# Batch 1's k and q between the halves of w_out, an earlier gate for w_in, and stores on SyncE: chunked attention with a snake MLP on one core

## The chip, the core and the metric

The kernel runs on one core of a Trainium2 chip. The metric is device time in microseconds (us), from the first to the last instruction of the core. Before the change the median of three runs is 218.45 us (217.29 to 218.61). Profiles are single executions with the hardware profiler on; that of the kernel before spans 218.0 us.

The engines are TensorE (PE in the profile; its weight loads are PEld), VectorE (DVE), ScalarE (ACT), GpSimd (POOL) and SyncE (SP). SyncE issues transfers only. GpSimd issues transfers too, and all loads that convert float32 to bf16 go through it. Each of the two has one queue of its own, in program order: an instruction that waits holds all behind it.

## The reference

Four batches of eight heads attend in chunks of 32 queries, each to 16 positions to the left, 8 to the right and 8 memory positions. The result, as 3072 rows of 512, goes through two matrix products with a "snake" function between them.

```python
def _attn_ref(q, k, v, mem_k, mem_v):          # q, k, v: (4, 8, 768, 64); mem: (4, 8, 8, 64)
    chunk, left_ctx, right_ctx = (32, 16, 8)
    scale = 1.0 / np.sqrt(D)
    for c in range(S // chunk):
        ...                                     # l_start, r_end: the chunk with its context
        k_full = np.concatenate([mem_k, k[:, :, l_start:r_end]], axis=2)
        v_full = np.concatenate([mem_v, v[:, :, l_start:r_end]], axis=2)
        scores = scale * np.matmul(q_c, k_full.transpose(0, 1, 3, 2))
        a = np.exp(scores - scores.max(-1, keepdims=True))
        out[:, :, c_start:c_end] = np.matmul(a / (a.sum(-1, keepdims=True) + 1e-09), v_full)

def _moe_ref(x, w_in, w_out, alpha):            # x: (3072, 512), w_in: (512, 2048), w_out: (2048, 512)
    h = x @ w_in
    s = np.sin(alpha * h)
    return (h + s * s / (alpha + 1e-09)) @ w_out
```

## The kernel before

The program runs batch by batch: attention of batch 0, layer 0 (the first product and the snake), then for each later batch its attention, into which the second product of the batch before is fed a few matmuls at a time, and its layer. Attention works in 8 blocks of 96 queries. The order of instructions is set by hand.

Attention of batch 0, with the gate for the weights and the later loads (cut):

```python
def attention_first(kq, alphas, ahead, load_weights, next_loads):
    ...
    pv(0, 0)
    put_k_edges(0, 2, t2)
    turn_q(2)                       # PE transposes, VectorE copies group 2 into qTs[0]
    warm(1)                         # a matmul of zeros that keeps TensorE busy
    pv(0, 1)
    t3 = turn(kq[0], 3, None)
    put_k(0, 3, t3)
    warm(1)
    x(0, 0)                         # PE transposes, ScalarE copies into xT[0]
    load_weights(xT)
    ...
    pv(1, 1)
    next_loads()
    ...
    ahead(0, xT, (4, 1))            # first half of the first product for groups 0, 1, 2
    ...
    ahead(2, xT, (0, 3))

def load_weights(xT):
    nc.gpsimd.tensor_copy(gate[:], xT[0][0:1, 0, 0:1])   # GpSimd waits for x(0, 0)'s copy
    for c in range(5):
        load_w_in(c)                # columns 0, 256, 512, 1024, 1536 to 2048 of w_in

def next_loads():
    for c in range(2):
        load_w_out(c)               # rows 0-1023, rows 1024-2047
    nc.gpsimd.dma_start(memv_st[64:72, 1:B].rearrange(...), mem_v[1:B].rearrange(...))
    kq1.extend(alloc_qk())
    load_qk(1, kq1, 0, H)           # k of batch 1, then q
```

What layer 0 starts besides its own work, and the way into batch 1's attention:

```python
def send_memv(b):                   # memory rows of v, one copy for each of 8 blocks
    for j in range(NJ):
        nc.sync.dma_start(vws[b % 2][64:72, :, j, 0:D], memv_st[64:72, b])

def begin_0(ft):
    if ft == 3:
        plan(h=[6] + rings["big"])
    if ft == 8:
        load_v(1)
    if ft == 12:
        send_memv(1)
        send_memv(2)
    if ft == 15:
        prs.extend(pair_up(kq1[n // HP], n % HP) for n in range(4))   # GpSimd copies of k

layer(0, xT, "PPPAVPAVAAVAVAAA", begin_0, 0)      # ends with second(0, ...) queued, cut = 13
last4 = rings["h"]
plan(one=(last4[0], last4[0] + 1), t=(last4[1], last4[1] + 1), big=last4[1:])
put_memk(1)
feed.take(20)                       # 20 matmuls of the second product
for pc in range(2 * HP):            # turn k's four pairs, then q's, 2 matmuls after each
    ...
nc.scalar.preload_act_table(ACTF.Exp)
load_v(2)
feed.take(4)
xT = attention(1, feed, (6, 8, 4, 4, 4, 3, 3, 3, 3, 2), 2, 5)
```

The attention of batches 1 to 3. `big` is a ring of three pairs of PSUM banks, which the scores of one block and the values of another take in turn:

```python
def attention(b, stream, shares, lag, crossed, ...):
    state["attending"] = True
    state["store"] = nc.gpsimd
    for s in range(NJ + lag + 1):
        if s < NJ:
            ptl[s] = scores(b, s)                  # 8 matmuls into a pair; ScalarE: exp
        stream.take(n // 2)
        j = s - lag
        state["copying"] = j >= NJ - 1
        if j >= NJ - 1:
            state["store"] = nc.sync
        ...
        if 0 <= j < NJ:
            xbl[j] = values(b, j, ptl.pop(j))      # 8 matmuls into a pair; VectorE: reciprocal, multiply
            if j < crossed:                        # blocks 0 to 4
                nc.sync.dma_start_transpose(block_of(xT, j), ...)
        stream.take(n - n // 2)
        ...

def end_o(s, bank):                                # end of 128 rows of the second product
    o_sb = mlp.tile([P, d_model], F32, name="o_sb", bufs=2)
    if (s % 2 == 0 or state["attending"]) and not state["copying"]:
        nc.vector.tensor_copy(o_sb[:], ps[:, bank, :])
    else:
        nc.scalar.copy(o_sb[:], ps[:, bank, :])
    state["store"].dma_start(out[...], o_sb[:])
```

`state["store"]` is SyncE at first. Layer 2 sets it to GpSimd at its step 12, ahead of batch 3's attention, in both kernels.

Of the kernel before, what the change touches and what calls it, by code (L numbers as in the profile page):

```python
# [9 lines left out]
P = 128  # L10
# [32 lines left out]
def kernel(  # L43
# [12 lines left out]
    nc = tc.nc  # L56
    B, H, S, D = q.shape
# [40 lines left out]
    def single(kind="one"):  # L98
        return ps[:, take_bank(kind), :]

    def packed(bank, n, width):
        return bank.bitcast(BF)[:, 0:n * width].rearrange("p (n c) -> p n c", n=n)
# [8 lines left out]
    qTs = [consts.tile([P, HP, S], BF, name=f"qT{i}") for i in range(2)]  # L111
# [11 lines left out]
    gate = consts.tile([1, 1], BF, name="gate")  # L123
# [6 lines left out]
    def alloc_qk():  # L130
        kb = qkst.tile([P, H, 6, D], BF, name="k_bf")
        qb = qkst.tile([P, H, 6, D], BF, name="q_bf")
        return kb, qb
# [37 lines left out]
    def load_qk(b, bufs, h0, h1):  # L171
        for src, dst in ((k, bufs[0]), (q, bufs[1])):
            nc.gpsimd.dma_start(
                dst[:, h0:h1].rearrange("p h r d -> p h (r d)"),
                src[b, h0:h1].rearrange("h (p r) d -> p h (r d)", p=P),
            )
# [49 lines left out]
    def load_w_out(c):  # L226
        nc.gpsimd.dma_start(
            w_out_sb[:, 8 * c:8 * c + 8, :],
            moe_w_out[1024 * c:1024 * c + 1024].rearrange("(ft p) o -> p ft o", p=P),
        )  # L230
# [10 lines left out]
    def turn(src, hp, pr):  # L241
        t = packed(single("t"), 6, P)
        for r in range(6):
            if pr is not None:
                nc.tensor.transpose(t[:, r, :], pr[:, r].rearrange("p e d -> p (e d)"), ident[:])  # L245
            else:
                for e in range(2):
                    nc.tensor.transpose(  # L248
                        t[64 * e:64 * e + 64, r, :], src[:, 2 * hp + e, r, :], ident[:]
                    )  # L250
        return t

    def put_k_edges(b, hp, t):
        kT = kTs[b % 2]
        for t0, c0 in ((0, 16), (120, 800)):
            nc.vector.tensor_copy(
                kT[:, hp, c0:c0 + 48].rearrange("p (a r) -> p a r", r=6),
                t[:, :, t0:t0 + 8].rearrange("p r a -> p a r"),
            )

    def put_k(b, hp, t):
        kT = kTs[b % 2]
        nc.scalar.copy(  # L263
            kT[:, hp, 72:72 + 7 * 104].rearrange("p (s c) -> p s c", c=104)[:, :, 0:96]
            .rearrange("p s (a r) -> p s a r", r=6),
            t[:, :, 8:120].rearrange("p r (s a) -> p s a r", a=16),
        )

    def put_q(b, hp, t, scalar=False):
        (nc.scalar.copy if scalar else nc.vector.tensor_copy)(  # L270
            qTs[b % 2][:, hp, :].rearrange("p (a r) -> p a r", r=6),
            t.rearrange("p r a -> p a r"),
        )
# [3 lines left out]
    state = {"n": 0, "attending": False, "copying": False, "store": nc.sync}  # L277
# [46 lines left out]
    def alloc_x():  # L324
        return [xp.tile([P, KT, HALF], BF, name=f"xT{hf}") for hf in range(2)]
# [15 lines left out]
    def warm(n):  # L341
        z = ps[:, rings["one"][0], :]
        for _ in range(n):
            nc.tensor.matmul(z, idle[:, 0:P], idle[:])  # L344
# [53 lines left out]
    def attention_first(kq, alphas, ahead, load_weights, next_loads):  # L398
        xT = alloc_x()
        pt, xb = {}, {}  # L400

        def turn_k(hp):
            t = turn(kq[0], hp, None)
            put_k(0, hp, t)
            put_k_edges(0, hp, t)

        def turn_q(hp):
            put_q(0, hp, turn(kq[1], hp, None))

        def sc_half(hp, half):  # L410
            pt[hp, half] = unit_scores(hp, half)

        def sc(hp):
            for half in range(2):
                sc_half(hp, half)

        def pv(*u):
            xb[u] = unit_values(*u, pt[u])

        def x(hp, half, copy=nc.scalar.copy):  # L420
            unit_turn(xT, hp, half, xb.pop((hp, half)), copy)

        turn_k(0)
        warm(2)
        turn_q(0)
        mt = packed(single(), HP, 32)
        for g in range(HP):
            nc.tensor.transpose(mt[:, g, :], memk_bf[0:32, 2 * g:2 * g + 2, :].rearrange("p e d -> p (e d)"), ident[0:32, 0:32])
        nc.vector.tensor_copy(memkT[:], mt)
        put_memk(0)  # L430
        warm(3)
        turn_k(1)
        put_memv(0, nc.vector, 0, H)
        warm(2)
        sc(0)
        turn_q(1)
        alphas()
        warm(3)
        sc(1)
        t2 = turn(kq[0], 2, None)  # L440
        put_k(0, 2, t2)
        pv(0, 0)
        put_k_edges(0, 2, t2)
        turn_q(2)
        warm(1)
        pv(0, 1)
        t3 = turn(kq[0], 3, None)
        put_k(0, 3, t3)
        warm(1)
        x(0, 0)  # L450
        load_weights(xT)
        sc_half(2, 0)
        put_k_edges(0, 3, t3)
        turn_q(3)
        sc_half(2, 1)
        x(0, 1)
        warm(1)
        plan(big=(4, 0, 2))
        pv(1, 0)
        sc_half(3, 0)  # L460
        pv(2, 0)
        sc_half(3, 1)
        pv(3, 0)
        x(1, 0)
        warm(1)
        x(2, 0)
        pv(1, 1)
        next_loads()
        warm(2)
        x(3, 0)  # L470
        nc.scalar.preload_act_table(ACTF.Sin)
        plan(big=(0, 2))
        pv(2, 1)
        ahead(0, xT, (4, 1))
        x(1, 1)
        pv(3, 1)
        ahead(1, xT, (5, 2))
        x(2, 1)
        ahead(2, xT, (0, 3))
        plan(big=(4, 0, 2))  # L480
        x(3, 1, nc.vector.tensor_copy)
        for ft in range(3):
            half_sine(ft, "PVP"[ft])
        return xT

    def attention(b, stream, shares, lag, crossed, beside=iter(()), beside_from=0):
        xT = alloc_x()
        ptl, xbl = {}, {}
        state["attending"] = True
        state["store"] = nc.gpsimd  # L490
        for s in range(NJ + lag + 1):
            n = shares[s] if s < len(shares) else 0
            if s < NJ:
                ptl[s] = scores(b, s)
            if s == NJ - 1:
                nc.scalar.preload_act_table(ACTF.Sin)
            stream.take(n // 2)
            if s >= beside_from:
                next(beside, None)
# [4 lines that stand above are left out]
            if j == NJ:  # L504
                ahead(1, xT)
                half_sine(1)
            if 0 <= j < NJ:
                xbl[j] = values(b, j, ptl.pop(j))
                if j < crossed:
                    nc.sync.dma_start_transpose(  # L510
                        block_of(xT, j), xbl.pop(j)[:].rearrange("p g e d -> p (g e d)")
                    )
            stream.take(n - n // 2)
            if j == NJ - 1:
                ahead(0, xT)
                half_sine(0)
            if crossed <= j - 1 < NJ:
                turn_x(xT, j - 1, xbl.pop(j - 1))
        ahead(2, xT)
        half_sine(2)  # L520
        state["attending"] = state["copying"] = False
        return xT
# [173 lines left out]
    for vw in vws:  # L696
        nc.vector.memset(vw[:, :, :, D:D + 1], 1.0)

    def load_weights(xT):
        nc.gpsimd.tensor_copy(gate[:], xT[0][0:1, 0, 0:1])  # L700
        for c in range(5):
            load_w_in(c)

# [4 lines left out]
        nc.vector.reciprocal(inv_alpha[:], alpha_sb[:])  # L708

    def next_loads():  # L710
        for c in range(2):
            load_w_out(c)
        nc.gpsimd.dma_start(memv_st[64:72, 1:B].rearrange("n b h d -> n (b h) d"),
                            mem_v[1:B].rearrange("b h n d -> n (b h) d"))
        kq1.extend(alloc_qk())
        load_qk(1, kq1, 0, H)

    feed = Feed()
    kq1 = []
    xT = attention_first(kq, alphas, ahead, load_weights, next_loads)  # L720


# [27 lines left out]
# [5 lines that stand above are left out]
        if ft == 12:  # L755
            send_memv(1)
            send_memv(2)
        if ft == 15:
            prs.extend(pair_up(kq1[n // HP], n % HP) for n in range(4))

    layer(0, xT, "PPPAVPAVAAVAVAAA", begin_0, 0)
# [18 lines left out]
    xT = attention(1, feed, (6, 8, 4, 4, 4, 3, 3, 3, 3, 2), 2, 5)  # L780

    for i in range(1, B):
# [28 lines left out]
        if not last:  # L811
# [3 lines left out]
            xT = attention(i + 1, feed, (4, 8, 4, 4, 3, 3, 3, 3, 4, 4, 4), 2, 5)  # L815
# [33 lines left out]
```

The softmax here doesn't subtract the row's maximum and nothing guards it: scores larger than these inputs give would overflow.

## Time and profile before

| What | Value |
|---|---|
| Time, median of 3 | 218.45 us |
| PE busy | 208.4 us |
| ACT busy | 154.2 us |
| DVE busy | 138.0 us |
| POOL busy | 82.5 us |
| POOL queue (q0): bytes moved | 16.64 MB in 71,792 packets |
| SP queue (q1): bytes moved | 10.03 MB in 26,328 packets |
| w_in loads issued by GpSimd | from 18.11 us |
| Batch 1's attention, first scores | 59.20 us |
| Batch 2's attention, first scores | 96.35 us |
| Output stores on SP / on POOL | 18 / 7 |

How to read the profile: a line of a timeline or of a chain of waits starts with the start in us from the beginning and the length in us, then the engine, the line of the kernel and the operation, as output<-input. "x16" is the number of instructions merged into the line. What stands in brackets is how long the engine was idle before, and what it had waited for. In a table of waits the numbers are the total in us, the number of times, and the longest. SPq and POOLq are the queues that issue transfers, which are not counted as busy time on SP. A DMA issue has the time to landing beside it: from the issue until all of it has arrived. Busy time of PE includes overlap of one matmul with the next, so small holes matter more than the percentage suggests.

### The profile page before, as it was taken

Reading aid. Unit: us, or ns where it says so; the run is one execution under the profiler, and the core shown is the slowest. Engines: PE = TensorE matmul, PEld = TensorE weight load, DVE = VectorE, ACT = ScalarE, POOL = GpSimd, SP = SyncE. Lnnn points to the kernel's source line nnn. Section 1 sums busy time; section 2 is a strip of 40 time slices with the busy share of each in tenths; the row PEclk is TensorE's granted clock in tenths of the full one; section 3 lists DMA queues with packets and bytes.
Section 4 is the critical chain, followed back from the end, with each engine's and each line's share of the span. In section 5 each row is a group of like instructions: output and inputs, shape, how many; then the busy total and the mean of one; then the engine's idle time right before and its main releaser. Section 6 shows DMA issues by size and latency. Waiting matters only on the chain.

```text
span 218.0 us, 4433 instructions
## 1 busy us (share of the span) xinstructions
PE 208.4 (96%) x1660; PEld 114.3 (52%) x1684; DVE 138.0 (63%) x246; ACT 154.2 (71%) x241; POOL 82.5 (38%) x108
## 2 busy tenths in 40 slices
PE   7989799999999999989999999999999999999994
PEld 2456556555545655644555555544555555544453
DVE  5767679994527789985756675665853753871110
ACT  2357879994778999998968778897876778651010
POOL 7987696208811599401168199111000000000000
PEclk9999999999999999999999999999999999999999
DMA  5999999999999599998529999997510110111212
GB/s 78 166 162 139 154 205 204 202 205 161 144 186 177 113 125 151 160 163 119 119 34 168 117 122 148 179 250 132 120 51 2 48 53 0 48 48 51 96 48 96
DMA packets 98141, 26.94 MB, mean 124 GB/s; under 512 B 86520, under 2 KB 95624, under 8 KB 98120
## 3 DMA queue, kind: packets, MB, share of 16 engines
q0 software_dynamic: 71792, 16.64, 89.0%
q1 hardware_dynamic: 26328, 10.03, 24.7%
q8 instruction: 13, 0.21, 0.4%
q14 instruction: 8, 0.07, 0.2%
HBM read 29.66 MB, written 6.29 MB: 165 GB/s over the span
## 4 chain that ended last, share of the span: by engine, by line
PE 74%; DVE 8%; ACT 6%; DMA 6%; issue 4%; POOL 0%; DVEq 0%; ACTq 0%
PE ps L597 33%; PE ps L528 28%; DVE gT L582 4%; ACT u L538 4%; DMA w_in_sb<-in_moe_w_in_dram 4%; PE ps L344 3%; PE ps L284 3%; PE ps L310 2%; DMA xT<-x_blk 2%; DVE u L552 2%; PE ps L620 2%; PE ps L248 1%; ACT kT L263 1%; PE ps L245 1%; DVE qT L270 1%
## 5 line engine op out<-in xcount | busy, mean ns | idle before, releaser
L597 PE MATMUL ps<-w_out_sb,gT 128*128 128x512 bf16 x347 | 91.6, 380 | 1.6 <-DVE gT L582 0.4
L528 PE MATMUL ps<-xT,w_in_sb 128*128 128x384 bf16 x512 | 90.9, 326 | 1.7 <-DMA w_in_sb<-in_moe_w_in_dram 1.0
L582 DVE SCALAR_TENSOR_TENSOR gT<-u,inv_alpha,ps 128x768 bf16<-128x768 f32 (+1 forms) x76 | 65.6, 885 | 19.8 <-ACT u L549 16.3
L538 ACT ACTIVATE u<-ps,alpha_sb 128x768 f32<-128x768 f32 (+1 forms) x76 | 59.6, 794 | 18.9 <-PE ps L528 18.5
L528 PEld LDWEIGHTS <-w_in_sb 128*128 128x128 bf16 x512 | 49.5, 98 | 38.3 <-issue 1.6
L597 PEld LDWEIGHTS <-gT 128*128 128x128 bf16 x368 | 32.7, 97 | 29.8 <-issue 1.3
L549 ACT ACTIVATE u<-u 128x768 f32<-128x768 f32 (+1 forms) x50 | 37.0, 741 | 1.6
L297 ACT ACTIVATE pt<-ps,biasm 128x256 bf16<-128x256 f32 x72 | 28.7, 472 | 5.0 <-PE ps L284 2.1
L610 DVE COPY o_sb<-ps 128x512 f32<-128x512 f32 x14 | 9.6, 689 | 26.7 <-PE ps L597 26.7
L613 POOL DMA_DIRECT2D out_dram<-o_sb x7 | 4.0, 569 | 41.4 <-DVE o_sb L610 25.2
L552 DVE TENSOR_TENSOR u<-u 128x768 f32<-128x768 f32 (+1 forms) x20 | 17.9, 893 | 1.7 <-ACT u L538 1.6
L184 POOL DMA_DIRECT2D vw<-in_v_dram x15 | 18.0, 1213 | 0.9 <-issue 0.9
L317 DVE TENSOR_TENSOR x_blk<-ps,rinv 96x512 bf16<-96x512 f32 x24 | 16.5, 687 | 0.8
L612 ACT COPY o_sb<-ps 128x512 f32<-128x512 f32 x9 | 5.2, 580 | 12.9 <-PE ps L597 12.9
L263 ACT COPY kT<-ps 128x672 bf16<-128x672 bf16 x8 | 5.7, 717 | 10.7 <-PE ps L248 7.9
L142 POOL DMA_DIRECT2D kst<-in_k_dram x16 | 11.3, 705 | 4.4 <-DMA vw<-in_v_dram 4.4
L147 POOL DMA_DIRECT2D kst<-in_k_dram x16 | 11.8, 740 | 0.5 <-DMA qst<-in_q_dram 0.3
L310 PEld LDWEIGHTS <-pt 128*128 128x128 bf16 x192 | 9.1, 98 | 4.3
L152 POOL DMA_DIRECT2D qst<-in_q_dram x12 | 10.9, 911 | 1.0 <-DMA vw<-in_v_dram 1.0
L284 PEld LDWEIGHTS <-kT 64*128 64x128 bf16 x192 | 4.9, 94 | 10.4 <-issue 9.5
L344 PE MATMUL ps<-idle 128*128 128x512 bf16 x24 | 8.9, 497 | 1.5 <-DVE vw L659 1.2
L316 DVE RECIPROCAL rinv<-ps 96x8 f32<-96x8 f32 x24 | 4.8, 202 | 8.2 <-ACT pt L297 5.2
(83 smaller groups left out, 146.2 us busy)
## 6 DMA issues: line engine op xcount, KB each, us to landing
out_dram<-o_sb SPq DMA_DIRECT2D x16, 256.0 KB
w_out_sb<-in_moe_w_out_dram POOLq DMA_DIRECT2D x2, 1024.0 KB, 19.5
out_dram<-o_sb POOLq DMA_DIRECT2D x7, 256.0 KB, 3.4
w_in_sb<-in_moe_w_in_dram POOLq DMA_DIRECT2D x3, 512.0 KB, 11.3
vw<-in_v_dram POOLq DMA_DIRECT2D x3, 512.0 KB, 8.9
qst<-in_q_dram POOLq DMA_DIRECT2D x12, 128.0 KB, 6.3
vw<-in_v_dram POOLq DMA_DIRECT2D x2, 448.0 KB, 17.4
kst<-in_k_dram POOLq DMA_DIRECT2D x14, 64.0 KB, 5.6
```

Of the source, the lines that this page charges most:

```text
L147: nc.gpsimd.dma_start(kst[72:72 + n, j, :].rearrange("p (h d) -> p h d", d=D), k[b, :, QW * j + 48:QW * j + 48 + n, :].rearrange("h p d -> ...
L184: nc.gpsimd.dma_start(vw[p0:p1, c0:c1, 0:D], flat[r0:r0 + QW * (c1 - c0)].rearrange("(n t) d -> t n d", t=QW)[0:p1 - p0],)
L297: nc.scalar.activation(pt[:, 0:H * QW].rearrange("p (g e c) -> p g e c", g=2, e=4)[:, :, :, 32 * m:32 * m + 32], sc[:, :, 0:4 * QW].rearra ...
L310: nc.tensor.matmul(otv[:, e, hp, :], pt[:, QW * i:QW * i + P], vws[b % 2][:, 2 * hp + e, j, 0:D + 1],)
L317: nc.vector.tensor_tensor(out=x_blk[:].rearrange("p g e d -> p e g d"), in0=otv[0:QW, :, :, 0:D], in1=rinv[:].unsqueeze(3).to_broadcast([Q ...
L344: nc.tensor.matmul(z, idle[:, 0:P], idle[:])
L528: nc.tensor.matmul(ps[:, bank, 0:HALF], w_in_sb[:, kt, P * ft:P * ft + P], xT[hf][:, kt, :], start=(kt == 0), stop=(kt == KT - 1),)
L538: nc.scalar.activation(u[:, e], hT, ACTF.Sin, scale=alpha_sb[:, ft:ft + 1])
L549: nc.scalar.activation(x, x, ACTF.Square)
L552: eng.tensor_tensor(out=x, in0=x, in1=x, op=ALU.mult)
L582: nc.vector.scalar_tensor_tensor(out=gT[:, ft, :].rearrange("p (e c) -> p e c", e=2)[:, e], in0=u[:, e], scalar=inv_alpha[:, ft:ft + 1], i ...
L597: nc.tensor.matmul(ps[:, bank, :], gT[:, ft, P * s:P * s + P], w_out_sb[:, ft, :], start=(ft == 0), stop=(ft == FT - 1),)
```

## The change

It has three parts. The weights' gate reads a column of qT (group 2, copied by VectorE) in place of the first column of xT, so that the w_in loads are held a shorter time. The k and q of batch 1, which were loaded behind both halves of w_out and the memory values, are loaded in turn with the halves: w_out 0, k, w_out 1, q, memory values; they should be there when GpSimd prepares the pairs, which is also begun one step earlier. And the attention no longer moves the output stores to GpSimd by itself: those of batches 1 and 2 stay on SyncE, those around batch 3's attention stay on GpSimd, by the line in layer 2.

```diff
@@ attention_first
         turn_q(2)
+        load_weights()
         warm(1)
         pv(0, 1)
         t3 = turn(kq[0], 3, None)
         put_k(0, 3, t3)
         warm(1)
         x(0, 0)
-        load_weights(xT)
@@ attention
         state["attending"] = True
-        state["store"] = nc.gpsimd
@@
-    def load_weights(xT):
-        nc.gpsimd.tensor_copy(gate[:], xT[0][0:1, 0, 0:1])
+    def load_weights():
+        nc.gpsimd.tensor_copy(gate[:], qTs[0][0:1, 2, 0:1])
         for c in range(5):
             load_w_in(c)
@@
     def next_loads():
-        for c in range(2):
+        kq1.extend(alloc_qk())
+        for c, src, dst in ((0, k, kq1[0]), (1, q, kq1[1])):
             load_w_out(c)
+            nc.gpsimd.dma_start(
+                dst[:].rearrange("p h r d -> p h (r d)"), src[1].rearrange("h (p r) d -> p h (r d)", p=P)
+            )
         nc.gpsimd.dma_start(memv_st[64:72, 1:B].rearrange("n b h d -> n (b h) d"),
                             mem_v[1:B].rearrange("b h n d -> n (b h) d"))
-        kq1.extend(alloc_qk())
-        load_qk(1, kq1, 0, H)
@@ begin_0
-        if ft == 15:
+        if ft == 14:
             prs.extend(pair_up(kq1[n // HP], n % HP) for n in range(4))
```

## The prediction

> **What bounds the kernel now.** I read the busy shares first, then the chain of work that ended last, then the waits of the DMA-issuing queues, then the timelines around the places where the change acts. Of the page:
>
> ```profile
> PE 208.4 (96%) x1660; PEld 114.3 (52%) x1684; DVE 138.0 (63%) x246; ACT 154.2 (71%) x241; POOL 82.5 (38%) x108
> ...
> PE 74%; DVE 8%; ACT 6%; DMA 6%; issue 4%; POOL 0%; DVEq 0%; ACTq 0%
> ```
>
> TensorE is busy in 96% of the span and carries 74% of the chain, so a saving must close one of its few holes, and a new hole is paid in full. The largest hole ahead of a load is in the chain between 17 and 30 us:
>
> ```profile
> 17.87 0.18 POOL gate L700
> 18.05 0.06 issue
> 18.11 0.77 POOL w_in_sb L221
> 18.88 7.74 DMA w_in_sb<-in_moe_w_in_dram
> 26.62 0.05 issue
> 26.66 0.82 PE ps L528 x4
> ```
>
> The columns are start, length and what ran. The tiny gate copy holds the w_in loads back until the first xT copy; the second load of w_in lands at 26.62 and TensorE, in the PE timeline, had nothing to do for 1.05 us before 26.66. The next lines are of the SyncE queue: who waited (its waits) and when it issued (its timeline):
>
> ```profile
> SPq L211 <- DMA memv_st<-in_mem_v_dram: 41.8, 1, 41.8
> ...
> 44.69 12.27 SPq L211 DMA_DIRECT2D vw<-memv_st  x16
> 57.05 1.03 SPq L613 DMA_DIRECT2D out_dram<-o_sb  x2
> 65.30 7.38 SPq L510 DMA_TRANSPOSE xT<-x_blk  x5
> ```
>
> The 16 sends of memory values (send_memv for batches 1 and 2) can't start before memv_st is loaded, take 12.27 us to issue, that is 0.767 us each, and the first output store stands right behind them in the same queue, at 57.05; its data (the copy of 56.31) had been ready since 56.99. Last, VectorE and TensorE around the start of batch 1's attention (their timelines):
>
> ```profile
> 56.31 0.68 DVE L610 COPY o_sb<-ps 128x512 f32<-128x512 f32 x1
> 56.98 0.96 DVE L270 COPY qT<-ps 128x768 bf16<-128x768 bf16 x1
> 61.79 0.69 DVE L610 COPY o_sb<-ps 128x512 f32<-128x512 f32 x1 [3.86 <-PE ps L597]
> 64.21 0.20 DVE L316 RECIPROCAL rinv<-ps 96x8 f32<-96x8 f32 x1 [1.73 <-ACT pt L297]
> 64.45 0.69 DVE L317 TENSOR_TENSOR x_blk<-ps,rinv 96x512 bf16<-96x512 f32 x1
> ...
> 65.65 0.38 PE L597 MATMUL ps<-w_out_sb,gT 128*128 128x512 bf16 x1
> 65.96 0.34 PE L284 MATMUL ps<-qT,kT 64*128 64x96 bf16 x8
> ```
>
> The copy at 61.79 is the third output copy. There are two o_sb buffers, so it needs the first store to have landed; now it waits only for its matmuls. The reciprocal and multiply behind it free the PSUM pair that the scores of block 4 (65.96) write. That order is what the change touches.
>
> **What the Trainium skill says.** "DMA: Bandwidth & Descriptors", section "Queues, rings and completion order": on each DMA engine descriptors are consumed in ring order. The trace agrees for the GpSimd queue: memv_st, only 24 KB, was issued at 23.56 and took 21.1 us to land, at 44.7, just behind the second half of w_out (issued some 22.7, 21.6 us, 44.3); k and q, issued behind it, took 24.3 and 25.2 us and landed at 48.5 and 52.4. So a small load at the end of that queue lands with the last large one. Same page, "Issuing engines are not separate DMA queues": transfers of SyncE and GpSimd run on the same DMA engines and interleave. The trace agrees: the packets of the first store, issued at 57.05, ran from 58.80 to 60.74 (3.7 us) amid v loads, while the store issued at 160.68 with little else going was through at 162.34 (1.7 us). "TensorE: Matmul & The Clock Gate", section "Part 1: The HAM clock gate": an idle window of about 3.4 us can halve the array's clock until it has been busy as long. The trace shows the slow state only at the start (the idle-fill matmuls take up to 635 ns against a least of 377).
>
> **The change part by part.**
>
> 1. *Gate earlier.* The gate now reads a column of qT, group 2, whose VectorE copy runs 15.92 to 16.86, instead of xT, whose ScalarE copy ended at 17.81. GpSimd has been free since 15.61, so w_in is issued about 1.0 us earlier. If it lands as much earlier, the hole of 1.05 us before 26.66 closes; as v of batch 0 is still arriving until about 20, I count 0.5 to 1.0 us earlier for everything on that queue.
>
> 2. *k and q between the halves of w_out.* The queue is full from w_in on (195 to 207 GB/s in every window from 28 to 48), so order is all that changes. Now: w_out 0 about 39, w_out 1 44.3, memv 44.7, k 48.5, q 52.4. After: k about 43, w_out 1 where k was, 48.5 less 0.3 for memv and less 0.5 to 1.0: about 47.5, q about 51.5, memv with it. Gains: the k pairs on GpSimd no longer wait 9.1 us (they start at 48.61 now), the q pairs come 0.5 to 1 us earlier, and the small holes of TensorE between 47 and 60.5 (13.5 less 12.93, 0.57 us) partly close. w_out 1 is needed at the ninth output matmul, 47.08 + 8 x 0.215 = 48.8, less the shift: just in time. Parts 1 and 2 together put TensorE at batch 1's attention about 1.3 us earlier.
>
> 3. *memv behind q.* This is the price. memv_st lands at about 51.7 (51.2 to 52.3) instead of 44.7. The 16 sends follow: 51.7 + 12.3 = 64.0. Only then the first store is issued, 7 us later than now. It lands 2.5 to 3.8 us on; I take 3.2, as the v load of batch 2 should be nearly through: 67.3. The third output copy waits for it, and so do all behind it on VectorE: copy 0.7 with its start, reciprocal 0.24, multiply 0.69, hand-over 0.15, 1.8 together: 69.1. The scores of block 4 can start then, against 65.96: +3.1 us. TensorE would have been there at about 64.7 by parts 1 and 2, so it stands for some 4.4 us, and their gain is swallowed: the start of block 4 no longer depends on them.
>
> 4. *Stores on SyncE in attention 1 and 2.* Two stores in each leave GpSimd (0.56 us each, 25.2 and 16.2 us of waiting in all its stores, none of it before work that anyone awaited: the gates at 73.10 and 110.09 waited for the xT copies). On SyncE they take 0.33 us of issuing each, in line with the transposes of x. In attention 2 I expect a small gain: TensorE waited 0.43 us at 110.95 for a transposed block issued at 106.23, whose straggling packets ran beside the GpSimd store of 107.07. I count -0.3. In attention 1 one more store precedes the first transpose and one stands between; VectorE's backlog delays them further; the fourth transpose was through at 71.9 for a first use at 73.08, 1.1 us of slack, which the order about uses up: +0.2.
>
> 5. *Pairs begun at step 14 instead of 15:* the order of GpSimd's instructions is the same, 0.
>
> 6. *Clock:* a hole of 4.4 us may contain an idle window; at half clock for some 3.4 us about 1.7 us would be lost (an estimate from the clock-gate page). At a third of a chance: +0.6.
>
> Sum: 3.1 - 0.3 + 0.2 + 0.6 = +3.6. I take 0.4 off for the waits of 0.2 to 0.9 us on ScalarE and VectorE in the attention that a late start absorbs: 218.45 + 3.2 = 221.7 us.
>
> **The rivals.**
>
> *The intended gain holds.* memv would have to land early, or the store not be held. Then parts 1, 2 and 4 give -1.3 - 0.3: 216.9 us. For it: TensorE is the bound and the 1.05 us hole is real. Against it: the 21.1 us that memv needed in the queue, and the 41.8 us that SyncE waited for just this load.
>
> *w_out 1 becomes the bound.* If k's 768-byte packets make the queue slower than counted, the ninth output matmul waits, by 0.5 us perhaps. It would be hidden behind step 3 in any case, and adds nothing.
>
> *The backlog costs more.* If the first store takes the 5.9 us that the second took now (57.7 to 63.54), or TensorE's clock falls for certain, block 4 starts at 71 to 72 or the rest of the attention runs at half pace: 223.5 to 225 us, slower by over 2%.
>
> *It is partly absorbed.* If the sends run faster when nothing else is queued, or the store lands within 1.7 us as at 160, block 4 starts at 67.5: 219.5 us.
>
> **Range and chances.** The terms that move the result are memv's landing (1 us), the store's landing (1.3 us), the clock (1.7 us) and the stage behind (1 us); together about 1.7 us either way of 221.7, with some room below for the first and last rivals: 218.7 to 224.3. The 2% lines are at 214.1 and 222.8. Below the first nothing reaches: 0.03. Above the second lie the upper end of the store and the clock: 0.27. Between: 0.70.
>
> **What would show it.** Step 1: TensorE's wait for w_in before the third group of ahead matmuls gone or under 0.5 us. Step 2: k pairs start near 43, q pairs near 51.7. Step 3: the sends start at 51 to 52.5 and end near 64, the first store is issued right behind them, the third o_sb copy is at 66.5 to 68.5 with an idle VectorE before it, and TensorE has a hole of 3.5 to 5.5 us before the scores of block 4. Step 4: no wait for transposed x in batch 2. Wrong it is if the sends start near 44, if the third copy follows its matmuls at once, or if TensorE fills the hole with other work.

## The result, and the profile after

The changed kernel takes 226.12 us (median of six runs, 225.67 to 227.0) against 218.06 us for the kernel before (217.29 to 218.61): a ratio of 1.038, with a 95% interval of 1.035 to 1.041. It is slower by 8.1 us, where 3.2 us had been predicted and 224.3 us was the upper end of the range. The order of events was the predicted one; two waits in it had not been foreseen, and the clock behind it cost more.

The page of the changed kernel, engines and chain. TensorE's work is the same and its share of the chain is down from 74% to 68%; what has come in is transfers (DMA, 6% to 8%) and GpSimd (POOL, 0% to 5%), most of it issuing loads:

```profile
PE 209.2 (93%) x1660; PEld 114.4 (51%) x1684; DVE 137.4 (61%) x246; ACT 154.2 (69%) x241; POOL 81.0 (36%) x104
...
PEclk9999999999995899999999999999999999999999
...
PE 68%; DVE 8%; DMA 8%; ACT 5%; POOL 5%; issue 4%; DVEq 0%; SPq 0%; POOLq 0%
```

The middle line is the granted TensorE clock in 40 slices. The 5 and the 8 stand for 67 to 78 us; the page of before shows no such slice. This was no accident of the traced execution: averaged over the span, all six granted 0.981 to 0.985 of the full clock.

The SyncE timeline of the changed kernel (start, length, what), to be held against the one of before, where the sends began at 44.69 and the first store at 57.05:

```profile
50.34 14.07 SPq L211 DMA_DIRECT2D vw<-memv_st  x16
65.26 4.82 SPq L612 DMA_DIRECT2D out_dram<-o_sb  x3
70.62 3.04 SPq L509 DMA_TRANSPOSE xT<-x_blk  x2
```

The 14.07 us are not all issuing. Taken in two windows, the sends go in two groups of eight, and the waits of the SyncE queue name what lies between the groups, and between them and the first store:

```profile
50.34 5.97 SPq L211 DMA_DIRECT2D vw<-memv_st  x8
58.24 6.17 SPq L211 DMA_DIRECT2D vw<-memv_st  x8
...
SPq L211 <- DMA vw<-memv_st: 1.8, 1, 1.8
SPq L612 <- DMA vw<-memv_st: 1.0, 2, 0.8
```

The ninth send waited 1.8 us for an earlier send to land, and the first store (L612) 0.8 us for another. In the first trace of before the second group follows the first at once (44.69 to 50.66, then 50.79 to 56.96).

The chain of waits of the changed kernel between 55 and 81 us:

```profile
58.24 6.96 DMA vw<-memv_st
65.20 0.02 issue
65.21 0.02 SPq L612
65.23 0.03 issue
65.26 3.65 DMA out_dram<-o_sb
...
69.03 0.06 DVE o_sb L609
69.09 0.55 issue
69.64 0.21 DVE rinv L316
69.84 0.02 issue
69.87 0.70 DVE x_blk L317
70.57 0.04 issue
70.61 0.51 PE ps L284 x8
```

It reads from top to bottom as one dependence after the other: the ninth send of memory values, issued at 58.24, lands at 65.20, SyncE goes on to the first output store at 65.26, that lands at 68.91, the third output copy (L609) starts on VectorE, then the reciprocal and the multiply, and the scores of block 4 (L284) at 70.61. The timelines show the two engines that stood still meanwhile, VectorE:

```profile
69.03 0.69 DVE L609 COPY o_sb<-ps 128x512 f32<-128x512 f32 x1 [11.87 <-DMA out_dram<-o_sb]
```

and TensorE, with the idle time and what ended it in brackets:

```profile
64.88 0.38 PE L596 MATMUL ps<-w_out_sb,gT 128*128 128x512 bf16 x1
70.61 0.51 PE L284 MATMUL ps<-qT,kT 64*128 64x96 bf16 x8 [5.35 <-DVE x_blk L317]
71.05 1.03 PE L596 MATMUL ps<-w_out_sb,gT 128*128 128x512 bf16 x2
...
80.68 9.62 PE L527 MATMUL ps<-xT,w_in_sb 128*128 128x384 bf16 x58
```

Two matmuls of 512 columns took 0.59 us before the hole and 1.03 behind it. The busy times by stage of the changed kernel (us, then PE, PEld, DVE, ACT and POOL busy with counts; the last three columns are the granted clock, the DMA share and GB/s) show why:

```profile
63.00:66.00 3.00, 2.21 (x30) 1.12 (x30) 0.00 (x0) 2.01 (x6) 0.00 (x0) 1.00 2.69 88
66.00:69.00 3.00, 0.00 (x0) 0.00 (x0) 0.00 (x0) 0.00 (x0) 0.00 (x0) 0.69 0.64 187
69.00:72.00 3.00, 1.39 (x12) 0.69 (x12) 2.29 (x5) 0.80 (x3) 0.00 (x0) 0.50 0.25 90
72.00:75.00 3.00, 3.00 (x38) 1.39 (x36) 1.87 (x5) 1.51 (x5) 0.00 (x0) 0.67 0.67 89
75.00:78.00 3.00, 2.95 (x48) 1.68 (x43) 2.23 (x6) 2.73 (x8) 0.00 (x0) 1.00 0.51 132
```

From 66 to 69 us no compute engine runs at all. The clock falls to 0.50 in the hole and is back at 1.00 by 75.

### The profile page after: what moved, and what is told of

Read it like the earlier page. It is cut to its first block, busy times and chain, and to the rows that moved or that the text cites. A ratio compares the mean times of both kernels' runs of the same rounds, so it can differ in the third digit from the quotient of the medians.

```text
span 223.9 us, 4432 instructions
## 1 busy us (share of the span) xinstructions
PE 209.2 (93%) x1660; PEld 114.4 (51%) x1684; DVE 137.4 (61%) x246; ACT 154.2 (69%) x241; POOL 81.0 (36%) x104
## 4 chain that ended last, share of the span: by engine, by line
PE 68%; DVE 8%; DMA 8%; ACT 5%; POOL 5%; issue 4%; DVEq 0%; SPq 0%; POOLq 0%
PE ps L596 32%; PE ps L527 27%; DVE gT L581 4%; ACT u L537 3%; POOL vw L184 3%; DMA vw<-memv_st 3%; DMA vw<-in_v_dram 3%; PE ps L284 3%; PE ps L310 2%; DVE u L551 2%; DMA out_dram<-o_sb 2%; PE ps L619 2%; ACT u L548 1%; POOL q_bf L173 1%; POOL k_bf L173 1%
## 5 line engine op out<-in xcount | busy, mean ns | idle before, releaser
L596 PE MATMUL ps<-w_out_sb,gT 128*128 128x512 bf16 x347 | 92.6, 383 | 1.7 <-DVE gT L581 0.7
L609 DVE COPY o_sb<-ps 128x512 f32<-128x512 f32 x14 | 9.6, 689 | 35.2 <-PE ps L596 23.3
L551 DVE TENSOR_TENSOR u<-u 128x768 f32<-128x768 f32 (+1 forms) x20 | 18.4, 921 | 1.9 <-ACT u L537 1.9
L284 PE MATMUL ps<-qT,kT 64*128 64x96 bf16 x192 | 8.6, 211 | 5.9 <-DVE x_blk L317 5.3
L284 PEld LDWEIGHTS <-kT 64*128 64x128 bf16 x192 | 5.1, 96 | 16.1 <-issue 15.3
L310 PE MATMUL ps<-vw,pt 128*128 128x65 bf16 x192 | 10.0, 195 | 0.0
```

Source lines behind the costliest of these rows:

```text
L284: nc.tensor.matmul(sc[:, e, QW * hp:QW * hp + QW], kTs[b % 2][64 * e:64 * e + 64, hp, pitch * j:pitch * j + P], qTs[b % 2][64 * e:64 * e + ...
L310: nc.tensor.matmul(otv[:, e, hp, :], pt[:, QW * i:QW * i + P], vws[b % 2][:, 2 * hp + e, j, 0:D + 1],)
L551: eng.tensor_tensor(out=x, in0=x, in1=x, op=ALU.mult)
L596: nc.tensor.matmul(ps[:, bank, :], gT[:, ft, P * s:P * s + P], w_out_sb[:, ft, :], start=(ft == 0), stop=(ft == FT - 1),)
```

## The experiments

The theory: the memory values, last in the GpSimd queue, hold the 16 sends on SyncE, these the first output store, this the third output copy (two buffers), this VectorE and with it TensorE. Rival A: the new order of k, q and w_out, or the earlier gate, is what costs. Rival B: the stores on SyncE cost, by holding transposes. All times are medians; each ratio is to the kernel before on the same chip, with its 95% interval.

| Run | Time, us | Ratio | Interval |
|---|---|---|---|
| before_again | 218.41 | (one run) | |
| memv_last | 226.40 | 1.032 | 1.026 to 1.037 |
| memv_first | 218.81 | 1.0004 | 0.998 to 1.003 |
| stores_only | 219.04 | 0.9987 | 0.996 to 1.001 |
| filled | 225.18 | 1.028 | 1.023 to 1.034 |
| three_o_sb | 222.87 | 1.018 | 1.013 to 1.023 |
| send2_later | 226.23 | 1.025 | 1.016 to 1.034 |
| gate_only | 218.92 | 1.0008 | 0.999 to 1.003 |
| memv_mid | 223.86 | 1.025 | 1.020 to 1.030 |
| old_gate | 218.76 | 1.0027 | 1.001 to 1.005 |
| candidate | 218.46 | 1.0006 | 0.999 to 1.002 |

The ratios leave out executions over 1.5% above the fastest of their kernel, so they don't follow exactly from the medians; in send2_later that leaves two of four.

**before_again: a second trace of the kernel before** (no edit).

> The kernel before once more, for a second profile. The changed kernel's traced span is only 5.9 us above that of the first trace of before (223.9 against 218.0), while the medians differ by 8.1 us. If the first trace was an unlucky execution, this one spans 216 to 217 us, with TensorE's hole in the batch 0 part smaller or the start earlier. If instead the profile hides part of the loss in the changed kernel, this spans 218 again.

Its span is 216.6 us, 1.4 us under the first trace, and the run took 218.41 us where the first traced run took 219.73. So the trace that the prediction was read from was a longer execution than most. TensorE's timeline of the second trace around 20 us, values matmuls of batch 0 and then the matmuls ahead:

```profile
19.86 0.40 PE L376 MATMUL ps<-vw,pt_first 128*128 128x65 bf16 x8 [0.43 <-DMA vw<-in_v_dram]
...
21.45 0.40 PE L376 MATMUL ps<-vw,pt_first 128*128 128x65 bf16 x8 [0.59 <-DMA vw<-in_v_dram]
...
25.33 0.82 PE L528 MATMUL ps<-xT,w_in_sb 128*128 128x384 bf16 x4
```

The wait of 1.05 us for w_in isn't there; instead TensorE waits twice for v, which it had not done in the first trace. The w_in loads were issued from 17.27, not 18.11. Block 4 of batch 1 starts at 64.61, not at 65.96. And the third output copy, in VectorE's timeline of this second trace, was already at the edge:

```profile
61.26 0.69 DVE L610 COPY o_sb<-ps 128x512 f32<-128x512 f32 x1 [4.67 <-DMA out_dram<-o_sb]
62.87 0.20 DVE L316 RECIPROCAL rinv<-ps 96x8 f32<-96x8 f32 x1 [0.91 <-ACT pt L297]
```

It waits for the first store even in the kernel before, and then VectorE still waits 0.91 us for exp: that is all the room there was for a later store.

**memv_last: the kernel before with the memory values behind k and q.**

```diff
     def next_loads():
         for c in range(2):
             load_w_out(c)
-        nc.gpsimd.dma_start(memv_st[64:72, 1:B]..., mem_v[1:B]...)
         kq1.extend(alloc_qk())
         load_qk(1, kq1, 0, H)
+        nc.gpsimd.dma_start(memv_st[64:72, 1:B]..., mem_v[1:B]...)
```

> The kernel before with one edit: the memory values are loaded behind k and q, nothing else of the change. Queue theory (late memory values hold SyncE, the first output store, the third output copy and with it VectorE and TensorE): memory values land at 51.5 to 52.5, sends end near 66, scores of block 4 at 71 to 73, 224 to 228 us, with a stretch at half clock. Rival A (the new order of k, q and w_out, or the earlier gate, is what costs): 217.5 to 219 us. Rival B (the stores moved to SyncE cost, by holding transposes): 217.5 to 219 us.

226.40 us, against 218.76 for the kernel before on that chip: 7.6 of the 8.1 us, from a load of 24 KB moved by two places. Sends from 50.64, the third copy at 69.50 after 12.71 us of waiting for the store, block 4 at 71.07 after a hole of 6.19 us, and the clock at 0.50 to 0.52 until 77. Rivals A and B fall: none of their parts is in this kernel.

**memv_first: the changed kernel with the memory values loaded first.**

```diff
     def next_loads():
+        nc.gpsimd.dma_start(memv_st[64:72, 1:B]..., mem_v[1:B]...)
         kq1.extend(alloc_qk())
         for c, src, dst in ((0, k, kq1[0]), (1, q, kq1[1])):
             ...
-        nc.gpsimd.dma_start(memv_st[64:72, 1:B]..., mem_v[1:B]...)
```

> The changed kernel with one edit: the memory values are issued ahead of the halves of w_out. Queue theory: the whole loss goes, sends end by 50, no hole at block 4, 215.5 to 217.5 us, so somewhat under before. Rival A (order or gate): 222 us or more. Rival B (stores on SyncE): 221 us or more.

218.81 us: the loss is gone, so the theory holds from both sides. But there is no gain (1.0004), where 215.5 to 217.5 us had been expected. In its trace the sends run from 32.77 to 45.04 and the k pairs start at 41.80; TensorE waits 0.78 and 0.79 us for v of batch 0, and the second product starts at 46.68, later than in the second trace of before (45.73).

**stores_only: the kernel before with the stores of attention 1 and 2 on SyncE.**

```diff
         state["attending"] = True
-        state["store"] = nc.gpsimd
```

> The kernel before with one edit: the stores of attention 1 and 2 stay on SyncE. Queue theory: 217.5 to 218.5 us, with the wait of 0.43 us for transposed x in batch 2 gone. Rival B: transposes held behind stores, 220 us or more.

No difference that the runs can show. In the trace the expected detail is there: the two traces of before have TensorE waiting for transposed x in batch 2's attention, 0.43 and 0.34 us, and this one has no such wait.

**filled: the changed kernel with 24 matmuls of zeros in the hole.** It adds work and leaves nothing out.

```diff
             n = shares[s] if s < len(shares) else 0
+            if b == 1 and s == 4:
+                for _ in range(24):
+                    nc.tensor.matmul(ps[:, rings["big"][1], :], idle[:, 0:P], idle[:])
             if s < NJ:
```

> The changed kernel with 24 matmuls of zeros (some 0.215 us each, 5.2 us) put ahead of the scores of block 4 of batch 1, where TensorE stands idle from 65.2 to 70.6; they need only block 3's exp, so they fill the hole. Clock theory: the array keeps its full clock, block 4 still starts near 70.6, the attention behind it loses the extra 1.5 us: 224 to 225 us against 226.1, granted clock 1.00. Rival (the slow stretch is the backlog on VectorE, not the clock): 226 us or more.

225.18 us, 0.9 us less than the changed kernel although it executes more (1.6 us less when each is held against the kernel before on its own chip); one stage of its busy times, same columns as above, shows the clock kept:

```profile
69.00:72.00 3.00, 3.00 (x28) 1.41 (x26) 2.31 (x6) 0.50 (x2) 0.00 (x0) 1.00 0.36 134
```

Block 4 starts at 71.06, and the long run of layer matmuls at 79.70: 8.64 us, against 10.07 in the changed kernel (70.61 to 80.68) and 8.69 in the second trace of before (64.61 to 73.30). So the half clock costs 1.4 us, and VectorE's backlog next to nothing. Between the two traced executions it isn't all gained, as block 4 itself came 0.45 us later here, and TensorE waits 0.59 us for transposed x in batch 3.

**three_o_sb: the changed kernel with three output buffers.**

```diff
-            o_sb = mlp.tile([P, d_model], F32, name="o_sb", bufs=2)
+            o_sb = mlp.tile([P, d_model], F32, name="o_sb", bufs=3)
```

(in all four places that share the buffers)

> The changed kernel with three output buffers instead of two; the order of every engine is the same. Queue theory: the third output copy no longer waits for the first store, but the fourth does (store landed at 68.9), so the hole moves from block 4 to block 6 of batch 1 and shrinks from 5.4 us to 2 to 3 us, too short for the half clock: 221 to 223 us. Rival (what holds VectorE or TensorE is not the buffer, but for example late memory rows of v at the values matmuls): 226 us, the hole stays at block 4.

222.87 us, in the range. VectorE's timeline of this kernel, output copies:

```profile
60.91 0.69 DVE L609 COPY o_sb<-ps 128x512 f32<-128x512 f32 x1 [3.86 <-PE ps L596]
...
69.14 0.69 DVE L609 COPY o_sb<-ps 128x512 f32<-128x512 f32 x1 [3.40 <-DMA out_dram<-o_sb]
```

The third copy now waits for its matmuls only, and the fourth takes the wait: TensorE's hole is 2.81 us, ahead of the scores at 70.72, which are those of block 6. The link through the buffer is shown. The expected full clock didn't come: it is at 0.50 from 71.25 to 74.66 us.

**send2_later: eight of the sixteen sends moved behind batch 1's attention.**

```diff
             send_memv(1)
-            send_memv(2)
@@
     xT = attention(1, feed, (6, 8, 4, 4, 4, 3, 3, 3, 3, 2), 2, 5)
+    send_memv(2)
```

> The changed kernel with the eight sends for batch 2 issued after batch 1's attention, so that only eight stand ahead of the first store; memory values stay last in their queue. Queue theory: sends end near 57.4, the first store lands by 61 to 63, the third copy waits under 1 us, 217.5 to 219.5 us. Rival (the late landing of the memory values themselves holds batch 1's values matmuls): 222 us or more.

Missed: 226.23 us, with executions from 222.54 to 227.32. The traced one is the fastest. Its chain of waits:

```profile
50.26 7.37 DMA vw<-memv_st
57.63 0.02 issue
57.65 0.02 SPq L612
57.66 0.05 issue
57.71 6.61 DMA out_dram<-o_sb
```

The sends were issued by 56.23, as expected, but the store then waited for one of them to land, to 57.63, and took 6.61 us itself, amid the v loads of batch 2, so that the third copy came at 64.44 and block 4 at 66.02 after a hole of 1.10 us. The moved sends then stand ahead of the loads for batch 2, and TensorE waits for transposed x three times (0.69, 1.34 and 0.60 us). The time falls into the rival's range, but the values matmuls, which the rival means, don't wait in this trace. Only this execution was traced. The mean granted clock of the others is 1.0 at 225.87 us, 0.992 at 226.58 and 0.985 at 227.32 (0.999 in the traced one). So two of them lost clock as the kernels with a long hole did, and the one of 225.87 us did not; what set it back stays open.

**memv_mid: the memory values between w_out 1 and q,** in the changed kernel.

```diff
             load_w_out(c)
+            if c == 1:
+                nc.gpsimd.dma_start(memv_st[64:72, 1:B]..., mem_v[1:B]...)
             nc.gpsimd.dma_start(dst..., src[1]...)
-        nc.gpsimd.dma_start(memv_st[64:72, 1:B]..., mem_v[1:B]...)
```

> The changed kernel with the memory values between w_out 1 and q: a dose between early and last. Queue theory: they land near 47.5, sends end near 60, the first store is issued at 60 to 61 and lands at 63 to 66, amid the v loads of batch 2, the third copy waits 3 to 5 us and TensorE has a hole of 0 to 2 us at block 4, at full clock: 218.5 to 221.5 us. Rival (a threshold: any memory value behind k costs the whole 8 us): 225 us or more.

223.86 us, above the range, and between early and last: a dose, no threshold. Its SyncE timeline:

```profile
46.98 13.29 SPq L211 DMA_DIRECT2D vw<-memv_st  x16
60.37 7.53 SPq L612 DMA_DIRECT2D out_dram<-o_sb  x3
```

Sends as expected. But the store issued at 60.37 took 6.36 us to land, the third copy came at 66.85, the hole is 3.44 us, and the clock is 0.58 from 69 to 72. Landing and clock were too kindly estimated once more. Of its four executions the fastest, 222.0 us, kept the clock (0.999); the others granted 0.992 (223.33 us) and 0.985 (224.38 and 225.03).

**gate_only: the kernel before with the earlier gate alone.**

```diff
+        load_weights()          # behind turn_q(2)
...
-        load_weights(xT)        # behind x(0, 0)
...
-        nc.gpsimd.tensor_copy(gate[:], xT[0][0:1, 0, 0:1])
+        nc.gpsimd.tensor_copy(gate[:], qTs[0][0:1, 2, 0:1])
```

> The kernel before with only the earlier gate for w_in. Theory from the traces: w_in's packets run beside the last v loads of batch 0 and delay them, TensorE's wait for w_in becomes waits for v of together 1.0 to 1.6 us, the first output matmul starts at 46.2 to 46.8 against 45.7 in the second trace of before: ratio 1.000 to 1.005. Rival (as predicted): the hole closes, ratio 0.995 to 0.997.

1.0008: no gain. The w_in loads are issued from 16.32; TensorE waits 0.21 and 0.83 us for v, as expected, but the second product starts at 45.76, as in the second trace of before (45.73) and not half a us later. All thirteen traces together tell more. In the four where w_in is issued before 16.7 us, TensorE waits 0.7 to 1.6 us for v. In the five where it is issued between 17.1 and 17.4, three have no such wait, one 0.21 us and one 1.02 us. In the four others, from 18.1 us on, v is not waited for. The wait for w_in stands in the first trace of before alone, although three more traces issue it as late. That the packets of w_in delay those of v fits this, and was not tried by itself.

**old_gate: the changed kernel with the memory values first and the gate of before** (the edits of memv_first, and those of gate_only undone).

> The changed kernel with the memory values ahead of w_out and the gate back at xT: what is left of the change is the order w_out 0, k, w_out 1, q and the stores on SyncE. It is the version that should be best, if anything here is. If the order brings nothing (the pairs were not awaited in an ordinary execution of before) and the stores a quarter of a us: ratio 0.997 to 1.000. If the order is worth what I had predicted for holes between 47 and 60 (0.57 us at most) on top: 0.995 to 0.997.

1.0027, slightly slower than before, outside both expectations. No gain from the order of k, q and w_out can be seen here; it was not tried apart from the other edits. The second product starts at 45.86 and the run of layer matmuls at 73.81, 0.5 us later than in the second trace of before; 0.27 us of it is a wait for transposed x in batch 1.

**candidate: the kernel before with the memory values first, its stores on SyncE and three output buffers.**

> A version meant to beat both: the kernel before with its gate and its order of w_out, k and q, but the memory values loaded first, the stores of attention 1 and 2 on SyncE, and three output buffers. If SyncE's backlog and the two buffers cost before nothing in an ordinary execution, as its second trace suggests (no wait of the third copy), only the removed wait for transposed x counts: ratio 0.997 to 1.000. If they cost something now and then: 0.993 to 0.997.

1.0006: no gain. The expectation misread the second trace of before: its third copy did wait for the first store (61.26, above). Here that copy waits for its matmuls only, and it brings nothing. Nor is the wait for transposed x gone: TensorE waits 0.49 us in batch 2 and 0.25 us in batch 1. No version tried here beats the kernel before.

## Why the prediction was right or wrong

The direction and its cause were right, the size was not: within 2% had been given 0.70, slower by over 2%, as it came, 0.27. Three terms of the sum failed: step 3 let the sends and the store follow each other without waiting for earlier sends to land (2.6 us), it counted from a block 4 that was 1.35 us late in the one trace read, and step 6 put the slow clock at 0.6 us where it took 1.4. The terms, with block 4 in the kernel before as in its second trace:

| Term | Predicted | Measured |
|---|---|---|
| memory values landed, sends start | 51.7 | 50.34 |
| 16 sends issued, without the wait, us | 12.3 | 12.3 |
| ninth send waits for an earlier one to land, us | none | 1.8 |
| last send to first store, us | 0.05 | 0.85 |
| first store to landing, us | 3.2 | 3.65 |
| copy, reciprocal, multiply to block 4, us | 1.8 | 1.70 |
| block 4 starts | 69.1 | 70.61 |
| block 4 in the kernel before | 65.96 | 64.61 |
| lost to the clock behind it, us | 0.6 | 1.4 |

1. *Step 3, memory values behind q,* was right as a mechanism in every link, and memv_last and memv_first settle it from both sides. What failed in it is "The 16 sends follow: 51.7 + 12.3 = 64.0. Only then the first store is issued". The issuing took what had been predicted, but the ninth send and the first store waited 1.8 and 0.8 us for earlier sends to land, and the prediction had no term for that. Block 4 is nevertheless only 1.5 us later than predicted, because the memory values landed 1.4 us earlier. That was luck: their landing too had been read from the longer trace, and in the second trace of before the sends start at 43.55, not at 44.69.

2. *The base of that step* was mis-sized by 1.35 us: the start of block 4 before was read from one trace, and there it came 1.35 us later than in the second. Against the second trace the loss at block 4 is 6.0 us, not 3.1.

3. *Step 6, the clock,* was counted at a third of a chance. It came in every traced kernel with a hole of 2.8 us or more, and cost 1.4 us (filled). The Trainium skill's window of about 3.4 us ("TensorE: Matmul & The Clock Gate", section "Part 1: The HAM clock gate") had made me expect the hole of three_o_sb to be too short; 2.81 us was enough. The clock fell at 71.25, behind 3.41 us in which TensorE was busy for 0.60; in the changed kernel it fell at 67.16, behind 3.41 us with 1.46 busy. So the page's length agrees with the traces, but the stretch need not be idle throughout.

4. *The 0.4 us taken off,* for waits that a late start absorbs, has no counterpart: from the run of layer matmuls to the end it is 143.2 us in the changed kernel and 143.3 in the second trace of before. Together 6.0 + 1.4 - 0.1 = 7.3 us, which is the difference of these two spans, 223.9 and 216.6. Reckoned from the predicted 3.2 us: 1.5 for the later block 4, 1.35 for the base, 0.8 for the clock, 0.4 and 0.1 for the reductions here and in step 4 that did not show, less the 0.1 just named, again about 7.3. The remaining 0.8 us of the 8.06 between the medians is where the two traced runs lie: 225.67 is 0.45 under its median, 218.41 is 0.35 over.

5. *Steps 1 and 2, the gains,* were wrong as gains. The hole of 1.05 us belonged to one execution; in the second trace it is two waits for v at the end of the same queue, and in the four other traces with the old gate neither is there. The earlier gate yields 1.0008, the order of k and q nothing that can be seen (old_gate). The k pairs did start earlier, 40.48 against 48.61, but TensorE had not been waiting for them. That their gain is swallowed by step 3 was right, but there was none to swallow.

6. *Step 4, the stores,* came to about the -0.1 us it was given: nothing measurable. Its links are loose. With the stores on SyncE the wait for transposed x in batch 2 is gone in the changed kernel and in stores_only, but not in candidate (0.49 us), and it is missing in memv_last too, where the stores are on GpSimd. The wait in batch 1 that step 4 feared is there in old_gate and candidate (0.27 and 0.25 us).

7. *The rivals.* The intended gain did not come even with the memory values first (memv_first); the late w_out 1 showed no wait on TensorE in the changed kernel; and "the backlog costs more" is what happened, through the clock, as it named, and through waits of the sends, which it did not, and not through a store of 5.9 us. Its figure, 223.5 to 225 us, still fell short, as it was counted from the same late block 4.

## What to carry to other kernels

A small load put last in a full queue lands with the last large one; before moving it, follow what waits for it through the queue of the engine that does the waiting, as everything behind it there, needed or not, is late as well. Here 24 KB cost 8 us by way of 16 sends, one store and a buffer. Count not only how long that queue issues, but also how long it may wait for its own earlier transfers. Read at least two traces of the kernel before: a hole of 1 us seen in one of them may not be in the next, and a change made to close it closes nothing. When TensorE is going to stand for some 3 us, count the slow clock behind the hole in full.

## What the runs showed of the hardware that was not expected

Issuing a send of 8 KB took SyncE 0.685 us (the median in all thirteen traces), and with the gaps between them 16 sends occupied its queue for 12.3 us where none waited. The Trainium skill ("DMA: Bandwidth & Descriptors", section "Issuing engines are not separate DMA queues") calls the time to initiate a DMA usually small beside the DMA itself. For one send the trace agrees (0.685 us, and 6.96 us from issue to landing for the ninth in the changed kernel); it is the sum over 16, with the two waits, that held the store.

A transfer of SyncE waited for a send eight places ahead of it to land, though it needed nothing from it. In the changed kernel the first store waited for the ninth send (issued at 58.24, landed at 65.20), in memv_last likewise (58.10 to 65.23), and in send2_later, with eight sends ahead of it, for the first (50.26 to 57.63). Whether the chip or the program's semaphores set this distance stays open.

A store of 256 KB landed 3.65 us after its issue at 65.26, but needed 6.36 and 6.61 us at 60.37 and 57.71, with more of v of batch 2 still to load (it landed at 68.1, 68.5 and 66.9). An earlier store was not earlier by as much where it met such loads.

TensorE's clock was at 0.50 for 3.41 us with holes of 2.81 and 3.44 us, and for 6.83 us, twice as long, with holes of 5.35 and 6.19 us.
